# Who issues the stores, who narrows the weights, and how many staging buffers feed three chained layers on one core

## The chip, the core and the metric

The kernel runs on one core of one Trainium2 chip. The metric is the device time of one execution in microseconds. Before the change it is 679.35 us, the median of three runs (678.56 to 679.99). The core has a matrix engine (TensorE, "PE" in the profile, its weight loads "PEld"), a vector engine (VectorE, "DVE"), a scalar engine (ScalarE, "ACT"), a general engine (GpSimd, "POOL") and SyncE ("SP"), which in this kernel only issues transfers. Each engine runs its own list of instructions strictly in order and waits on semaphores for the others.

## The reference, cut to what matters

Three layers follow each other. The first is a spectral layer on x [4, 3072, 256]:

```python
X = np.fft.rfft(x, axis=1)
Yr = Xr @ w_r - Xi @ w_i + b_r
Yi = Xr @ w_i + Xi @ w_r + b_i
Yr = np.sign(Yr) * np.maximum(np.abs(Yr) - 0.01, 0.0)      # Yi the same
y = np.fft.irfft(Yr + 1j * Yi, n=3072, axis=1)
```

The second sends each of the 12,288 rows to the best of 8 experts, which keeps its first 384 rows; an expert is two matrices with a relu between (256 to 1024 to 256), and the result is scaled by the gate. Rows that no expert keeps are zero. The third layer is `h = x @ w_in; (h * sigmoid(h)) @ w_out` with 2048 hidden columns, on every row; it gives zero for a zero row. `w_in` and `w_out` arrive as 64-bit floats and are used at 32-bit precision.

## The kernel before, in words

Because the experts fill up early, the kernel transforms batch 0 and the first 1024 rows of batch 1, routes them, and takes a second, long branch only if some expert was not full. In the timed run that branch is not taken.

The order of work is this. `s1` (L347) transforms x by matmuls with a small table and stores the partial result to DRAM (`a_d`). `kphase` (L384) reloads it four frequencies at a time (`ar`), applies the second half of the transform (tile `xp`), the complex weights (`yp`), the bias and the shrinking (`y`, `cl`, on VectorE), and the first half of the inverse (`bp`), copies that out (`bo`, ScalarE) and stores it to DRAM (`b_d`). `is2` (L555) reloads it (`br`), finishes the inverse, stores the rows (`attn`), and computes the gate; `route`, `rank` and `slots` build the table of which row goes to which expert. For batch 1 only a third of that is needed (`third`), and it runs in between the first experts.

Each expert is a `first_ffn` (L960, 96 full-rate matmuls into `hp` and `y`, 8 steps) and a `second_ffn` (L997, the third layer for the expert's 384 rows, tiles `h`, `sg`, `gh`, `gl`, `o`). `experts` (L849) runs them in the order first 0, 1, 2, second 0, 1, 2, first 3, 4, second 3, 4, and so on. `gather` fetches an expert's rows (`xg`) by indirect transfers that GpSimd issues, and VectorE scales them by the gate; `turn` transposes them (`gtp`) into `xT`. `weights` (L929) brings an expert's weights in eight loads of 256 KB into staging tiles `st`.

For accuracy nearly every matmul is done as three, on a high part and a low part of each operand (`mm3`, L197). `split` (L187) makes the two parts: the high part is a rounding copy, the low part a subtraction (L191). A two-letter argument names the engines: "av" is ScalarE then VectorE, "ap" ScalarE then GpSimd. In `weights` the first matrix of an expert goes "av", the second "ap".

`narrow` (L796) turns a [128, 512] block of 64-bit floats, loaded into `nt`, into 32-bit ones in `na` with integer operations on VectorE. Its argument `bits` chooses how the sign is put back: for `w_in` ScalarE computes a sign and GpSimd multiplies by it; for `w_out` VectorE masks the sign bit (tile `nsg`) and joins it in.

The output is cleared first: `zero_out` (L203) issues one of 48 stores of 256 KB of zeros per call; finished rows are then scattered over it. `ZERO` (L40) places 16 of these calls in the second half of the spectral layer, and `experts` the others in each `second_ffn` after the first.

A scheduler with a timeline model of its own orders the instructions of each engine; `after` adds an order between two instructions without a wait. All transfers but the indirect ones are issued by SP, in one list.

Of the kernel before, what the change touches and what calls it, by code (L numbers as in the profile page):

```python
# [22 lines left out]
DFF = 2048  # L23
# [11 lines left out]
OWN = 2,  # L35
HEAD = 2
PMS = "vav"
HELD = 10
FULL = 0, 1, 3, 5, 7, 9, 11, 13, 15
ZERO = {}, {k: 2 for k in range(4, 20, 2)}, {}, {}  # L40
BIG = 65536.0
# [113 lines left out]
class Kernel:  # L155
    def __init__(self, ctx, tc, i, o):
        self.tc, self.nc, self.i, self.o = tc, tc.nc, i, o
        nc = self.nc
        cst = ctx.enter_context(tc.tile_pool(name="cst", bufs=1))
        self.dr = ctx.enter_context(tc.tile_pool(name="dr", bufs=1, space=bass.MemoryType.DRAM))  # L160
        self.ident = cst.tile([P, P], F32, name="ident")
        make_identity(nc, self.ident)
        self.table = cst.tile([P, NF, SC * E], F32, name="table")
        self.carry = cst.tile([P, E], F32, name="carry")
        nc.gpsimd.memset(self.carry, 0.0)
        nc.gpsimd.memset(self.table, 0.0)
# [7 lines left out]
        self.stored = {}  # L174

    def after(self, ins, first):
# [69 lines left out]
    def near(self):  # L246
# [4 lines left out]
        with self.stream("a", 3, "right"), self.sums("a", 2):  # L251
            self.warm()
            mix([self.s1(0, ads)], [1])
            spectra = self.kphase(0, ads, True)
            next(spectra)
            mix([self.load_tables(), spectra, self.s1(1, ads), self.ffn_in()], [8, 12, 20, 10], lead=[9, 3, 0, 0])
            with self.tc.issue_after(self.stored[1][-1]):
                self.route_consts()
            rest = self.kphase(1, ads, True)
            for _ in range(1 + HEAD):  # L260
                next(rest)
            mix([self.is2(0, (0, 1, 2), self.res)], [1])
# [122 lines left out]
    def kphase(self, b, ads, ahead=False):  # L385
# [38 lines left out]
        def shrink(k, xk, xo):  # L424
# [13 lines left out]
            v.tensor_scalar(cl, y, LAM, -LAM, ALU.min, ALU.max)  # L438
            v.tensor_tensor(cl, y, cl, ALU.subtract)
            return cl  # L440

        def back(k, bo, cl):
# [4 lines left out]
            if k % KG + 2 == KG:  # L447
                nc.sync.dma_start(out=b_d[k + 2 - KG:k + 2].rearrange("k p c -> p k c"), in_=bo)

# [5 lines left out]
        for k in range(0, NK + 6, 2):  # L455
# [6 lines left out]
            if k >= 6:  # L462
                if (k - 6) % KG == 0:
                    bo = kp.tile([P, KG, D], F32, tag="bo", name="bo")
                back(k - 6, bo, y.pop(k - 6))
            for _ in range(ZERO[b].get(k, 0)):
                self.zero_out()
            yield
# [94 lines left out]
    def is2(self, b, qbs, res):  # L563
# [17 lines left out]
        def rows(g):  # L581
# [4 lines left out]
            for z in range(0, LD, CH):  # L586
# [6 lines left out]
                nc.scalar.copy(aof[:nq, sl], pt[:nq])  # L593
            nc.sync.dma_start(out=od[:, :, g], in_=aof[:nq].rearrange("q (u c) -> q u c", c=D))
            return ao
# [199 lines left out]

    def narrow(self, src, n, bits):  # L796

# [5 lines left out]
        for sv, dv in src:  # L803
            nc.sync.dma_start(out=t[:, dv], in_=sv.bitcast(I32).rearrange("p (n z) -> p n z", z=2))
        low, high = t[:, :, 0], t[:, :, 1].bitcast(F32)
# [3 lines left out]
        nc.scalar.activation(a, high, AF.Abs, scale=UP)  # L809
        v.tensor_scalar(a, a, F_MIN, F_MAX, ALU.max, ALU.min)  # L810
        if bits:
            sg = pool.tile([P, n], I32, tag="nsg", name="nsg", bufs=1)
            v.tensor_scalar(sg, t[:, :, 1], -0x80000000, None, ALU.bitwise_and)
            v.scalar_tensor_tensor(u, u, 3, sg, ALU.logical_shift_left, ALU.bitwise_or)
            v.scalar_tensor_tensor(u, low, 29, u, ALU.logical_shift_right, ALU.bitwise_or)
        else:
            sg = pool.tile([P, n], F32, tag="nsg", name="nsg", bufs=1)
            nc.scalar.activation(sg, high, AF.Sign)
            v.tensor_scalar(u, u, 3, None, ALU.logical_shift_left)
            v.scalar_tensor_tensor(u, low, 29, u, ALU.logical_shift_right, ALU.bitwise_or)  # L820
            nc.gpsimd.tensor_tensor(a, a, sg, ALU.mult)
        return a

    def ffn_part(self, src, dst, bits):
        W = 512
        if self.i["moe2_w_in"].dtype == mybir.dt.int64:
            a = self.narrow(src, W, bits)
        else:
# [5 lines left out]
    def ffn_in(self):  # L834

        W = 512
        for q in range(8):
            h, z = q % 2, (q // 2) * W
            self.ffn_part([(self.i["moe2_w_in"][h * P:(h + 1) * P, z:z + W], slice(0, W))],
                          [self.wi[:, k, h, z:z + W] for k in range(2)], False)  # L840
            yield

    def ffn_out(self):
        for q in range(8):
            rows = [(self.i["moe2_w_out"][(2 * q + u) * P:(2 * q + u + 1) * P, :], slice(u * D, (u + 1) * D)) for u in range(2)]
            self.ffn_part(rows, [self.wo[:, k, 2 * q:2 * q + 2].rearrange("p j d -> p (j d)") for k in range(2)], True)
            yield

    def experts(self, again=False):  # L849
# [45 lines left out]
        for at, ph in enumerate(order):  # L895
# [7 lines left out]
            if ph < E:  # L903
                part = self.first_ffn(ph, xs.pop(ph), ws.pop(ph), ys)
            else:
                part = self.second_ffn(ph - E, ys.pop(ph - E))
            for _ in part:
                n += 1
                while due is not None and due <= n:
                    due = next(side, None)  # L910
                if n % 3 == 0:
                    next(fw, None)
                if ph > E and n % 2:
                    self.zero_out()
            if after < E:
                xs[after] = self.turn(xg.pop(after))

# [11 lines left out]
    def weights(self, s):  # L929
# [41 lines left out]
    def first_ffn(self, e, xT, ws, ys):  # L971
# [5 lines left out]
        for j in range(NJ + 1):  # L977
            if j < NJ:
# [6 lines left out]
                nc.scalar.activation(hh, hp, AF.Relu)  # L985
                nc.vector.scalar_tensor_tensor(hl, hp, 0.0, raw(hh), ALU.max, ALU.subtract)  # L986
                hs[j] = hh, hl
# [10 lines left out]
    def second_ffn(self, e, yT):  # L998
# [40 lines left out]
        for s_ in range(SC):  # L1039
# [56 lines left out]
```

## Time and profile before

| | |
|---|---|
| median of three runs | 679.35 us |
| profiled execution | 678.36 us, of it 676.5 us span on the engines |
| TensorE matmul | 630.6 us busy, 93% of the span, 4050 instructions |
| VectorE | 322.7 us, 48% |
| ScalarE | 316.3 us, 47% |
| GpSimd | 130.1 us, 19% |
| mean granted TensorE clock | 0.97 of full speed |
| moved by DMA | 83.1 MB, 123 GB/s over the span |

The profiled execution's own time is its span and 1.9 us around it. It lies 1.0 us under the median of the runs. TensorE is busy nearly all the time, so what counts is where it stands idle, where it runs at a lower granted clock, and what it waits for there. Matmuls overlap in the records (a new one starts before the last has drained), so the busy time of a stretch hides short pauses; the number of matmuls in it shows them. The other engines matter only where TensorE waits for them.

### The profile page before, as it was taken

Reading aid. Unit: us, or ns where it says so; the run is one execution under the profiler, and the core shown is the slowest. Engines: PE = TensorE matmul, PEld = TensorE weight load, DVE = VectorE, ACT = ScalarE, POOL = GpSimd, SP = SyncE. Lnnn points to the kernel's source line nnn. Section 1 sums busy time; section 2 is a strip of 40 time slices with the busy share of each in tenths; the row PEclk is TensorE's granted clock in tenths of the full one; section 3 lists DMA queues with packets and bytes.
Section 4 is the critical chain, followed back from the end, with each engine's and each line's share of the span. In section 5 each row is a group of like instructions: output and inputs, shape, how many; then the busy total and the mean of one; then the engine's idle time right before and its main releaser. Section 6 shows DMA issues by size and latency. Waiting matters only on the chain. (4 is left out here: it accounts for less than half of the span.)

```text
span 676.5 us, 10845 instructions
## 1 busy us (share of the span) xinstructions
PE 630.6 (93%) x4050; PEld 585.3 (87%) x4050; DVE 322.7 (48%) x637; ACT 316.3 (47%) x643; POOL 130.1 (19%) x121
## 2 busy tenths in 40 slices
PE   8699899899996989999999998999999899999993
PEld 4387789899984749899999997999999799999993
DVE  3369865675795684963222233442234442223330
ACT  4456533554233553464455444364544464544450
POOL 1036300000017531350001024220104220102001
PEclk7789999999996989999999999999999999999997
DMA  9997865786517795345000012750003320000000
GB/s 245 321 290 240 259 190 162 208 264 196 179 63 225 211 294 182 94 126 170 9 17 9 16 32 96 239 160 13 25 1 96 121 81 1 24 2 24 0 1 29
DMA packets 63542, 83.10 MB, mean 123 GB/s; under 512 B 4948, under 2 KB 53144, under 8 KB 63480
## 3 DMA queue, kind: packets, MB, share of 16 engines
q1 hardware_dynamic: 61176, 76.02, 36.7%
q0 software_dynamic: 2304, 6.29, 3.0%
q8 instruction: 34, 0.56, 0.4%
q14 instruction: 28, 0.23, 0.1%
HBM read 49.79 MB, written 32.51 MB: 122 GB/s over the span
## 5 line engine op out<-in xcount | busy, mean ns | idle before, releaser
L191 DVE TENSOR_TENSOR gl<-sg,gh 128x384 fp32r<-128x384 f32 x118 | 67.1, 572 | 163.3 <-ACT gh L183 163.1
L1019 ACT ACTIVATE sg<-h 128x384 f32<-128x384 f32 x128 | 62.5, 491 | 100.0 <-PE h L201 99.1
L200 PE MATMUL o<-wo,gl 128*128 128x256 f32 x354 | 92.7, 282 | 0.0
L201 PE MATMUL o<-wo,gh 128*128 128x256 f32 x354 | 92.4, 282 | 0.0
L199 PE MATMUL h<-yT,wi 128*128 128x384 f32 x256 | 86.1, 336 | 0.4 <-ACT yT L183 0.4
L200 PE MATMUL h<-yT,wi 128*128 128x384 f32 x256 | 86.1, 336 | 0.0
L201 PE MATMUL h<-yT,wi 128*128 128x384 f32 x256 | 85.5, 336 | 0.0
L199 PE MATMUL o<-wo,gh 128*128 128x256 f32 x354 | 73.3, 283 | 0.0
L201 PEld LDWEIGHTS o<-wo,gh 128*128 128x128 f32 x354 | 67.1, 190 | 0.0
L200 PEld LDWEIGHTS o<-wo,gl 128*128 128x128 f32 x354 | 67.0, 189 | 0.1
L183 ACT CAST gh<-sg 128x384 fp32r<-128x384 f32 x118 | 60.2, 514 | 10.5 <-PE o L201 7.4
L183 ACT CAST w<-st 128x512 fp32r<-128x512 f32 x64 | 39.2, 619 | 49.2 <-DMA st<-in_moe_w 47.0
L191 POOL TENSOR_TENSOR w<-st,w 128x512 fp32r<-128x512 f32 x32 | 42.4, 1326 | 91.0 <-ACT w L183 83.5
L199 PEld LDWEIGHTS o<-wo,gh 128*128 128x128 f32 x354 | 59.8, 188 | 0.0
L199 PE MATMUL yp<-wri,xk 128*128 128x256 f32 x188 | 55.8, 298 | 0.6 <-ACT xk L414 0.6
L200 PE MATMUL yp<-wri,xk 128*128 128x256 f32 x188 | 54.5, 290 | 2.0 <-DVE xk L415 1.5
L201 PE MATMUL yp<-wri,xk 128*128 128x256 f32 x188 | 53.2, 283 | 0.0
L986 DVE SCALAR_TENSOR_TENSOR hl<-hp,hh 128x384 fp32r<-128x384 f32 x64 | 34.6, 551 | 34.8 <-ACT hh L985 32.8
L985 ACT ACTIVATE hh<-hp 128x384 fp32r<-128x384 f32 x64 | 30.8, 489 | 41.6 <-PE y L200 18.5
L199 PEld LDWEIGHTS h<-yT,wi 128*128 128x128 f32 x256 | 48.3, 189 | 0.7 <-ACT yT L183 0.7
L199 PE MATMUL hp<-xT,w 128*128 128x384 f32 x128 | 45.6, 357 | 3.2 <-ACT xT L183 3.2
L200 PEld LDWEIGHTS h<-yT,wi 128*128 128x128 f32 x256 | 48.1, 188 | 0.0
(224 smaller groups left out, 1329.5 us busy)
## 6 DMA issues: line engine op xcount, KB each, us to landing
st<-in_moe_w SPq DMA_DIRECT2D x64, 256.0 KB, 3.0
out<-zt SPq DMA_DIRECT2D x48, 256.0 KB, 3.8
a_d<-ao SPq DMA_DIRECT2D x16, 384.0 KB, 4.0
ar<-a_d SPq DMA_DIRECT2D x12, 512.0 KB, 8.4
b_d<-bo SPq DMA_DIRECT2D x12, 512.0 KB, 3.1
br<-b_d SPq DMA_DIRECT2D x16, 384.0 KB, 4.9
xt<-in_x SPq DMA_DIRECT2D x15, 384.0 KB, 8.1
nt<-in_moe_w_in SPq DMA_DIRECT2D x8, 512.0 KB, 4.5
```

What stands on the lines that cost most here:

```text
L183: self.nc.scalar.copy(dst, src)
L191: e.tensor_tensor(dst, src, raw(hi), ALU.subtract)
L199: first = nc.tensor.matmul(out, lh, rh, start=start, stop=False)
L200: nc.tensor.matmul(out, ll, rh, start=False, stop=False)
L201: return first.ins, nc.tensor.matmul(out, lh, rl, start=False, stop=stop).ins
L985: nc.scalar.activation(hh, hp, AF.Relu)
L986: nc.vector.scalar_tensor_tensor(hl, hp, 0.0, raw(hh), ALU.max, ALU.subtract)
L1019: nc.scalar.activation(sg, hp, AF.Silu)
```

## The change

1. The stores of `b_d` and of `attn` in `is2` are issued by ScalarE in place of SP.
2. `HEAD`, two further steps of batch 1's spectra that ran ahead of `is2` for batch 0, goes.
3. No zeros are stored in the spectral layer. `experts` calls `zero_out` twice per step of `second_ffn` 0 and on every second step of the later ones.
4. `narrow` always uses the form with the sign bit on VectorE. Its loads are ordered behind the latest `ar` load, and its second operation behind the latest shrinking (`w_in`) or the latest low part of `hp` (`w_out`).
5. Four `st` buffers in place of two, and all low parts of the expert weights on VectorE.
6. `turn` of the next expert is called two steps before the end of a phase, not after it. Three `oo` buffers in place of two.

```diff
@@ near
-            for _ in range(1 + HEAD):
-                next(rest)
+            next(rest)
@@ kphase
-            v.tensor_tensor(cl, y, cl, ALU.subtract)
+            self.shrunk = v.tensor_tensor(cl, y, cl, ALU.subtract).ins
-                nc.sync.dma_start(out=b_d[k + 2 - KG:k + 2].rearrange("k p c -> p k c"), in_=bo)
+                nc.scalar.dma_start(out=b_d[k + 2 - KG:k + 2].rearrange("k p c -> p k c"), in_=bo)
-            for _ in range(ZERO[b].get(k, 0)):
-                self.zero_out()
@@ is2
-            nc.sync.dma_start(out=od[:, :, g], in_=aof[:nq].rearrange("q (u c) -> q u c", c=D))
+            nc.scalar.dma_start(out=od[:, :, g], in_=aof[:nq].rearrange("q (u c) -> q u c", c=D))
@@ narrow
-            nc.sync.dma_start(out=t[:, dv], in_=sv.bitcast(I32).rearrange("p (n z) -> p n z", z=2))
+            ins = nc.sync.dma_start(out=t[:, dv], in_=sv.bitcast(I32).rearrange("p (n z) -> p n z", z=2))
+            self.after(ins.ins, self.fetched)
-        v.tensor_scalar(a, a, F_MIN, F_MAX, ALU.max, ALU.min)
-        if bits:
+        first = v.tensor_scalar(a, a, F_MIN, F_MAX, ALU.max, ALU.min)
+        if after:
+            self.after(first.ins, after)
...
-        else:
-            sg = pool.tile([P, n], F32, tag="nsg", name="nsg", bufs=1)
-            nc.scalar.activation(sg, high, AF.Sign)
-            v.tensor_scalar(u, u, 3, None, ALU.logical_shift_left)
-            v.scalar_tensor_tensor(u, low, 29, u, ALU.logical_shift_right, ALU.bitwise_or)
-            nc.gpsimd.tensor_tensor(a, a, sg, ALU.mult)
@@ experts
-                if ph > E and n % 2:
-                    self.zero_out()
-            if after < E:
-                xs[after] = self.turn(xg.pop(after))
+                if ph >= E:
+                    for _ in range(2 if ph == E else n % 2):
+                        self.zero_out()
+                if m == last - 2 and after < E:
+                    xs[after] = self.turn(xg.pop(after))
@@ weights
-                st = self.mq.tile([P, 2, D], F32, tag="st", name="st", bufs=2)
+                st = self.mq.tile([P, 2, D], F32, tag="st", name="st", bufs=4)
-                self.split("ap" if m else "av", w[:, 0], w[:, 1], st)
+                self.split("av", w[:, 0], w[:, 1], st)
@@ second_ffn
-            oo = self.mc.tile([P, D], F32, tag="oo", name="oo", bufs=2)
+            oo = self.mc.tile([P, D], F32, tag="oo", name="oo", bufs=3)
```

Three places show how the lists of instructions move. The first is VectorE's list where the spectra of batch 1 end and the first expert begins: `dsts` is the last table of `slots`, `xg` are gathered rows being scaled, `w_...` low parts of expert weights, `xT` the low part of the first transposed rows. Before:

```order
L758 CAST dsts<-slbs 128x9
L436 TENSOR_TENSOR y<-yp,bias 128x512
L438 TENSOR_SCALAR cl<-y 128x512
L439 TENSOR_TENSOR cl<-y,cl 128x512
L191 TENSOR_TENSOR w_2190<-st,w_2190 128x512
L959 TENSOR_SCALAR xg<-xg,gws 128x256 x3
L191 TENSOR_TENSOR xT<-gtp,xT 128x384 x2
```

Now, from the third low part after `dsts` (the first two are those of `w_2166` and `w_2171`):

```order
L190 TENSOR_TENSOR w_2176<-st,w_2176 128x512
L952 TENSOR_SCALAR xg<-xg,gws 128x256
L434 TENSOR_TENSOR y<-yp,bias 128x512
L190 TENSOR_TENSOR w_2181<-st,w_2181 128x512
L952 TENSOR_SCALAR xg<-xg,gws 128x256
L436 TENSOR_SCALAR cl<-y 128x512
L952 TENSOR_SCALAR xg<-xg,gws 128x256
L190 TENSOR_TENSOR w_2186<-st,w_2186 128x512
L437 TENSOR_TENSOR cl<-y,cl 128x512
L190 TENSOR_TENSOR w_2191<-st,w_2191 128x512
L952 TENSOR_SCALAR xg<-xg,gws 128x256
L190 TENSOR_TENSOR xT<-gtp,xT 128x384
```

One low part of weights stood ahead of the first `xT`, now six do, and the last shrinking has moved in between them.

The second is SP's list of transfers. Before, a piece among the loads of the first experts, where zeros stand between weight loads and row stores:

```order
L538 DMA attn_69<-ao_2429 32x512 x4
L943 ISA
L943 DMA st<-in_moe_w 128x2x256
L208 DMA out<-zt 256x1x256 x5
L943 ISA
```

Now, after the first weight load of expert 3 (`flagi` is the flag that decides the second branch, `nt` the last blocks of `w_out`):

```order
L936 DMA st<-in_moe_w 128x2x256
L1056 TENSOR_LOAD flagi
L1056 ISA x2
L800 DMA nt<-in_moe_w_out 128x512 x2
L207 DMA out<-zt 256x1x256 x45
L936 ISA
L936 DMA st<-in_moe_w 128x2x256
```

The zeros have left the loads of the first three experts; 45 of the 48 stand in one row ahead of seven loads of expert 3.

The third is VectorE's list in the spectra of batch 0 (numbers kept; `xk`, `y` and `cl` belong to the spectra, `na`, `nt` and `nsg` to the narrowing of `w_in`). Before:

```order
L413 TENSOR_TENSOR xk_473<-xp_474,xk_473 128x4x128
L810 TENSOR_SCALAR na_713<-na_713 128x512
L415 TENSOR_TENSOR xk_473<-xk_473,xp_474 128x4x64
L436 TENSOR_TENSOR y_508<-yp_483,bias_264 128x512
L819 TENSOR_SCALAR na_713<-na_713 128x512
L438 TENSOR_SCALAR cl_510<-y_508 128x512
L820 SCALAR_TENSOR_TENSOR na_713<-nt_711,na_713 128x512
L439 TENSOR_TENSOR cl_510<-y_508,cl_510 128x512
```

Now:

```order
L434 TENSOR_TENSOR y_505<-yp_480,bias_264 128x512
L436 TENSOR_SCALAR cl_507<-y_505 128x512
L811 TENSOR_SCALAR nsg_464<-nt_459 128x512
L437 TENSOR_TENSOR cl_507<-y_505,cl_507 128x512
L184 COPY ao1_520<-ps1_522 96x512
L807 TENSOR_SCALAR na_461<-na_461 128x512
L812 SCALAR_TENSOR_TENSOR na_461<-na_461,nsg_464 128x512
L411 TENSOR_TENSOR xk_538<-xp_539,xk_538 128x4x128
```

The narrowing is spread over more steps of the spectra, and each block now has an operation (`nsg`) that reads a freshly loaded `nt` between two operations of the spectra.

## Rows read from the trace of the kernel before

**Rows 1.** Windows: stretch in us, then length, busy time (instructions) by engine, clock, DMA.

```profile
0.00:44.00 44.00, 33.18 (x109) 20.46 (x110) 18.96 (x34) 22.41 (x43) 7.75 (x19) 0.77 0.96 286
44.00:100.00 56.00, 53.41 (x347) 44.33 (x346) 44.73 (x74) 28.51 (x53) 17.28 (x12) 1.00 0.75 236
192.00:220.00 28.00, 20.47 (x112) 17.49 (x111) 19.12 (x44) 10.47 (x25) 15.14 (x13) 0.82 0.53 155
236.00:258.00 22.00, 18.88 (x78) 13.28 (x78) 15.74 (x25) 10.25 (x20) 8.66 (x7) 0.84 0.98 301
212.00:310.00 98.00, 92.94 (x481) 80.89 (x481) 66.12 (x142) 49.25 (x98) 40.21 (x32) 0.93 0.63 188
310.00:400.00 90.00, 90.00 (x642) 90.00 (x641) 24.46 (x44) 43.93 (x92) 7.21 (x7) 1.00 0.08 26
```

**Rows 2.** TensorE's waits, whole run: total us, times, longest us.

```profile
PE y L199 <- ACT hh L985: 4.0, 3, 1.5
...
PE hp L199 <- ACT xT L183: 3.2, 3, 1.4
PE xp L401 <- DMA ar<-a_d: 2.6, 1, 2.6
```

**Rows 3.** Windows in the later first_ffn phases, same columns.

```profile
404.00:408.00 4.00, 4.00 (x25) 4.00 (x24) 2.44 (x5) 1.26 (x3) 0.91 (x1) 1.00 0.29 98
412.00:428.00 16.00, 12.10 (x66) 10.66 (x66) 7.07 (x13) 7.05 (x15) 7.83 (x7) 1.00 0.36 111
524.00:536.00 12.00, 9.12 (x50) 8.13 (x49) 5.33 (x10) 5.72 (x13) 2.57 (x2) 1.00 0.44 131
```

**Rows 4.** ScalarE's timeline, 419 to 421 us: start, length, what, idle before.

```profile
419.52 0.62 ACT L183 CAST w<-st 128x512 fp32r<-128x512 f32 x1 [2.83 <-DMA st<-in_moe_w]
420.05 0.47 ACT L183 CAST xT<-gtp 128x384 fp32r<-128x384 f32 x1
```

**Rows 5.** Tile st: min/median/max ns, first and last start; landing in us.

```profile
L191 DVE TENSOR_TENSOR w<-st,w x32: 674/692/1172, 205.1 to 617.3; 128x512 fp32r<-128x512 f32 x32
L191 POOL TENSOR_TENSOR w<-st,w x32: 1263/1292/1817, 209.9 to 622.1; 128x512 fp32r<-128x512 f32 x32
...
DMA to landing us min/median/max: 2.6/3.0/6.0
```

**Rows 6.** SP's timeline of transfers: start, length, what.

```profile
25.83 0.99 SPq L804 DMA_DIRECT2D nt<-in_moe_w_in  x2
27.75 1.39 SPq L395 DMA_DIRECT2D ar<-a_d  x2
...
68.22 0.38 SPq L448 DMA_DIRECT2D b_d<-bo  x1
...
201.79 4.59 SPq L943 DMA_DIRECT2D st<-in_moe_w  x3
```

**Rows 7.** Tile nsg: min/median/max ns of two narrowing operations on VectorE.

```profile
L813 DVE TENSOR_SCALAR nsg<-nt x8: 414/426/1457, 73.2 to 249.0; 128x512 int32<-128x512 int32 x8
L814 DVE SCALAR_TENSOR_TENSOR na<-na,nsg x8: 676/689/694, 73.7 to 249.8; 128x512 int32<-128x512 int32 x8
```

**Rows 8.** SP's own waits, whole run.

```profile
SPq L448 <- ACT bo L183: 38.2, 10, 8.8
```

**Rows 9.** VectorE's timeline, 208.5 to 210 us.

```profile
208.66 0.35 DVE L959 TENSOR_SCALAR xg<-xg,gws 128x256 f32<-128x256 f32 x1 [2.25 <-DMA xg<-attn,srcs]
209.55 1.79 DVE L959 TENSOR_SCALAR xg<-xg,gws 128x256 f32<-128x256 f32 x1 [0.53 <-DMA xg<-attn,srcs]
```

**Rows 10.** GpSimd's timeline from 209.9 us.

```profile
209.90 1.28 POOL L191 TENSOR_TENSOR w<-st,w 128x512 fp32r<-128x512 f32 x1
```

**Rows 11.** SP's timeline, two runs of zero stores.

```profile
253.27 3.45 SPq L208 DMA_DIRECT2D out<-zt  x5
...
305.72 7.09 SPq L208 DMA_DIRECT2D out<-zt  x9
```

**Rows 12.** VectorE's waits, whole run.

```profile
DVE nsg L813 <- DMA nt<-in_moe_w_out: 7.5, 3, 3.6
```

More of the change, by code (lines that the diff above doesn't have):

```diff
@@ L35 @@
 OWN = 2,
-HEAD = 2
 PMS = "vav"
@@ L39 @@
 FULL = 0, 1, 3, 5, 7, 9, 11, 13, 15
-ZERO = {}, {k: 2 for k in range(4, 20, 2)}, {}, {}
 BIG = 65536.0
@@ L174, in __init__ @@
         self.stored = {}
+        self.again, self.evicted = False, None
     def after(self, ins, first):
@@ L794, in wide, with narrow @@
         self.wi = mw.tile([P, 2, 2, DFF], FR, name="wi")
-    def narrow(self, src, n, bits):
+    def narrow(self, src, n, after):
         nc, pool = self.nc, self.mn
@@ L809, in narrow, with ffn_part @@
         nc.scalar.activation(a, high, AF.Abs, scale=UP)
-        v.tensor_scalar(a, a, F_MIN, F_MAX, ALU.max, ALU.min)
-        if bits:
-            sg = pool.tile([P, n], I32, tag="nsg", name="nsg", bufs=1)
-            v.tensor_scalar(sg, t[:, :, 1], -0x80000000, None, ALU.bitwise_and)
-            v.scalar_tensor_tensor(u, u, 3, sg, ALU.logical_shift_left, ALU.bitwise_or)
-            v.scalar_tensor_tensor(u, low, 29, u, ALU.logical_shift_right, ALU.bitwise_or)
-        else:
-            sg = pool.tile([P, n], F32, tag="nsg", name="nsg", bufs=1)
-            nc.scalar.activation(sg, high, AF.Sign)
-            v.tensor_scalar(u, u, 3, None, ALU.logical_shift_left)
-            v.scalar_tensor_tensor(u, low, 29, u, ALU.logical_shift_right, ALU.bitwise_or)
-            nc.gpsimd.tensor_tensor(a, a, sg, ALU.mult)
+        first = v.tensor_scalar(a, a, F_MIN, F_MAX, ALU.max, ALU.min)
+        if after:
+            self.after(first.ins, after)
+        sg = pool.tile([P, n], I32, tag="nsg", name="nsg", bufs=1)
+        v.tensor_scalar(sg, t[:, :, 1], -0x80000000, None, ALU.bitwise_and)
+        v.scalar_tensor_tensor(u, u, 3, sg, ALU.logical_shift_left, ALU.bitwise_or)
+        v.scalar_tensor_tensor(u, low, 29, u, ALU.logical_shift_right, ALU.bitwise_or)
         return a
-    def ffn_part(self, src, dst, bits):
+    def ffn_part(self, src, dst, after):
         W = 512
         if self.i["moe2_w_in"].dtype == mybir.dt.int64:
-            a = self.narrow(src, W, bits)
+            a = self.narrow(src, W, after)
         else:
@@ L839, in ffn_in @@
             self.ffn_part([(self.i["moe2_w_in"][h * P:(h + 1) * P, z:z + W], slice(0, W))],
-                          [self.wi[:, k, h, z:z + W] for k in range(2)], False)
+                          [self.wi[:, k, h, z:z + W] for k in range(2)], None if self.again else self.shrunk)
             yield
@@ L845, in ffn_out @@
             rows = [(self.i["moe2_w_out"][(2 * q + u) * P:(2 * q + u + 1) * P, :], slice(u * D, (u + 1) * D)) for u in range(2)]
-            self.ffn_part(rows, [self.wo[:, k, 2 * q:2 * q + 2].rearrange("p j d -> p (j d)") for k in range(2)], True)
+            self.ffn_part(rows, [self.wo[:, k, 2 * q:2 * q + 2].rearrange("p j d -> p (j d)") for k in range(2)], self.evicted)
             yield
@@ L903, in experts @@
             if ph < E:
-                part = self.first_ffn(ph, xs.pop(ph), ws.pop(ph), ys)
+                part, last = self.first_ffn(ph, xs.pop(ph), ws.pop(ph), ys), F // P
             else:
-                part = self.second_ffn(ph - E, ys.pop(ph - E))
-            for _ in part:
+                part, last = self.second_ffn(ph - E, ys.pop(ph - E)), DFF // P + 1
+            for m, _ in enumerate(part):
                 n += 1
@@ L985, in first_ffn @@
                 nc.scalar.activation(hh, hp, AF.Relu)
-                nc.vector.scalar_tensor_tensor(hl, hp, 0.0, raw(hh), ALU.max, ALU.subtract)
+                self.evicted = nc.vector.scalar_tensor_tensor(hl, hp, 0.0, raw(hh), ALU.max, ALU.subtract).ins
                 hs[j] = hh, hl
```

## The prediction

> **What bounds the kernel now.** I read the windows by stage first [rows 1]. From 310 to 400 us TensorE is busy for the whole stretch at full clock; no change can win anything there. It loses time in four places, and there is nothing else to win: the start (0 to 44, 33.2 us busy, granted clock 0.77), the first gather (192 to 220, 20.5 of 28, clock 0.82), a hole at 236 to 258 (18.9 of 22, clock 0.84, DMA busy 98%), and the two later `first_ffn` phases [rows 3]. In the stretches at 0.77 to 0.84 part of the time was spent at the lower of the two levels (1.2 GHz, not 2.4). Idle time and the lower level stand in the same windows, so an idle microsecond there may be paid twice, once as idle and again as slow matmuls.
>
> The second view is TensorE's list of waits [rows 2]: it stands for `hh` (4.0 us in 3), `xT` (3.2 in 3) and once 2.6 us for `ar`. The first two have ScalarE as releaser, so I looked at what ScalarE did before: a weight cast that had waited 2.83 us for the DMA of its `st` tile, with the `xT` cast queued behind it [rows 4]. The engine is not slow; it is held in order behind a late load.
>
> The third is SP's list [rows 6, 8, 11]: two `nt` loads go ahead of the first `ar`, three `st` issues take 4.59 us where zeros share the queues, and SP stands 38.2 us in ten waits for `bo`.
>
> **The change, part by part.** The sum is made against the profiled execution, 678.4 us (span 676.5 and 1.9 around it); the median is 1.0 higher, and I add that at the end.
>
> *Staging buffers and low parts (later phases).* A `st` buffer is held for the landing (3.0 us), ScalarE's cast (0.62) and the low part. For the second matrix the low part is GpSimd's, 1.29 us [rows 4, 5]: 4.9 us, and with two buffers one load per 2.46 us. Eight loads feed 96 matmuls, which at full pace (25 in 4 us) last 15.4 us, so one load is wanted every 1.9 us. The loads are the limit, and the holes are where they should be: 412 to 428 has 66 matmuls where 100 would fit, 524 to 536 has 50 of 75 [rows 3]. That is 34 and 25 missing at 0.16 us, 9.4 us in all; the idle time alone is 3.9 and 2.9, 6.8 us. After the change a buffer is held 3.0 + 0.62 + 0.69 = 4.3 us, and with four of them a load can come every 1.08 us, well under 1.9. What is late next is nothing on this path: VectorE is 44% busy in these windows (7.07 of 16), and four more low parts per expert add 2.8 us. I take 8 us of the 9.4 (a few matmuls at the edges are missing only by the count), range 5 to 9.4. The earlier `turn` and the third `oo` buffer act on the same holes and are counted here.
>
> *236 to 258, and the phases around it.* The nine zero stores (2.4 MB) issued by SP while DMA is busy 98% [rows 1, 11] go. Reachable are the idle 3.1 us and, at most, (1 - 0.84) x 22 = 3.5 us of clock: 6.6. Against it, VectorE gets here 12 low parts that were GpSimd's (12 x 0.69 = 8.3 us) and four more `w_out` blocks, each five operations between 0.43 and 0.69 us [rows 7], 2.2 us at least, so 9 us: 66 us busy of 98 becomes 83, 85%. An engine in order at 85% is late now and then: each low part of `hp` or `xT` that comes 0.7 us late behind a narrowing costs TensorE that, and seven such come to 5 us. I take a gain of 2, nearer to the middle, range -5 to +6.6.
>
> *Start, 0 to 44.* Loads of `w_in` now stand behind the latest `ar` load, so the two `nt` ahead of it (1 MB) [rows 6] go. At the 286 GB/s of this stretch [rows 1] 1 MB is 3.7 us; the wait for `ar` that it can shorten is 2.6 us [rows 2], and behind it (1 - 0.77) x 44 = 10 us went to the slow clock, most of it in the unavoidable first loads. I take 3, range 0 to 5.
>
> *44 to 100.* TensorE idles 2.6 us here [rows 1]. VectorE loses four `w_out` blocks (9 us) and gains the sign-bit form for `w_in`. Two of that form's operations are in rows 7, 1.1 us together; the shift and the join of the old form stay, so about one operation per block more, 0.43 to 0.69. The stores on ScalarE free SP of its 38.2 us of waiting [rows 8], during which the `ar` and `br` loads behind a store could not be issued. ScalarE pays the issue: 0.38 us a store where SP does it [rows 6], up to 0.7 by the `ar` and `st` loads there. Three stores of `b_d` stand in this stretch and 12 in the run, with 8 of `attn`: 1 to 2 us here, at most 14 in the run, on an engine that is 51% busy (28.5 of 56), hidden beside TensorE's 53 us of matmuls, and on the path if the copy behind a store is the one TensorE waits for. I take a gain of 1, range -3 to +2.6.
>
> What the row shows here is head-of-line waiting, 38.2 us on SP, up to 8.8 at a time [rows 8]. The Trainium skill (DMA: Bandwidth & Descriptors, "Issuing engines are not separate DMA queues") says that starting transfers from several engines saves only the sequencer's time for starting them, usually small beside the transfer. By that rule this term is 0 and the sum 1 us less. The rule does not count a wait ahead of the issue, and that is what the row has; which is right, the waits for `ar` and `br` after the change would show.
>
> *First gather, 192 to 220.* Idle 7.5 us and (1 - 0.82) x 28 = 5 us of clock [rows 1], the largest hole. It is made by the chain routing table, row gather, scaling, transposing, and the change doesn't touch its length except at two points. The scaling of one `xg` took 1.79 us in place of 0.35 while GpSimd did a low part beside it [rows 9, 10]; without GpSimd's work that is 1.4 us won. Against it, six low parts (6 x 0.69 = 4.1 us) stand on VectorE ahead of the first `xT` where one stood, and the fifth and sixth need a second turn of the buffers: from 201.8 (the first of the issues in rows 6), two turns of 4.3 us end at 210.4, and the last scaling before was done at 211.3 (209.55 + 1.79 [rows 9]). So they just fit, and if the loads land late (6.0 at worst, [rows 5]) `xT` is late by up to 4. I take 0.5, range -4 to +4. Two steps of batch 1's spectra that ran ahead of `is2` are no longer there (`HEAD`); they are moved, not removed, and are matmuls either way.
>
> *Zeros.* 45 stores stand on SP in one row ahead of seven loads of expert 3. At 7.09 us for 9 [rows 11] their issue lasts 35 us. DMA is busy 8% from 310 to 400 [rows 1], and those weights are wanted from about 400. Issued from about 310 they are through by 345, and the transfers (45 x 0.26 MB at 301 GB/s, 39 us) by 350: no cost. If SP got to them only after 355, the loads behind would come after 394 and each further microsecond would be one on TensorE.
>
> The sum: 8 + 2 + 3 + 1 + 0.5 = 14.5 us. 678.4 - 14.5 = 663.9, and with the 1.0 to the median 664.9 us.
>
> **The rivals.** *Only the weights.* The two later phases win 8, and the early terms come to nothing, since one hole there is filled by another: the start is bound by loads, the gather by its chain, and VectorE takes back what the DMA gives. 679.35 - 8 = 671.4. For it: the weights are the one term in which cause, period and hole agree; against it: the wait for `ar` has a plain cause in SP's order.
>
> *The early holes close and the clock stays up.* If the start, the hole at 236 and 44 to 100 all reach their upper bounds' better half, the clock does not fall either: 9 + 5 + 4 + 2 + 2.4 = 22.4, 657. All upper bounds together are 9.4 + 6.6 + 5 + 2.6 + 4 = 27.6, 651.8. For it: idle time and slow clock stand together in all three windows; against it: VectorE at 85% in the middle one.
>
> *VectorE held by fresh loads (slower).* The sign-bit operation `nsg` reads a freshly loaded `nt`, and now stands in order between operations of the spectra in all 16 blocks. Where it waited before it was 2.5 us each (7.5 in 3 [rows 12]). Sixteen such waits hold VectorE 40 us, and behind it stand `y`, `cl` and the low part of `xk`, for which TensorE waits. The kernel is slower than before from the point where over 14.5 + 1.4 = 15.9 us of these, 1.0 us per block, reach TensorE; if half of them do, 20 us, it is 664.9 + 20 = 684.9. Against it: most of the loads before had landed when the operation came (3 waits), and the order of the loads behind `ar` moves them away from the busiest moment, but later as well.
>
> **How the numbers follow.** The forecast 0.52; only the weights 0.24; the early holes 0.16; VectorE held 0.08, of which 0.06 is slower and 0.02 ends within the bound. What can be told from no change is 0.2%, 1.4 us. So faster 0.92, same 0.02, slower 0.06. The range that holds 8 in 10: its low end is the third case, 657, and 1 below it; its high end is the second, 671.4, with 3.6 for the low bounds of the early terms (the -4 of the gather). 656 to 675.
>
> **What would show it.** Weights: 100 matmuls in 16 us in the later `first_ffn` phases, and no wait for `hh` or `xT` behind ScalarE. Start: no 2.6 us wait for `ar`, and `nt` behind it on SP. Middle: DMA under 0.9 where it was 0.98, clock over 0.9, and VectorE near 85%; waits of TensorE for VectorE's low parts there would show my -5. Gather: all `xg` scalings at 0.35, and the first `xT` behind six low parts at no later time than before. Zeros: one row of 45 on SP, ended before 355. I am wrong if `nsg` shows waits in the spectra that TensorE's waits for `xk` or `y` repeat, or if ScalarE's issues of stores stand ahead of copies for which TensorE waits.

## The result and the profile after

The changed kernel takes 660.82 us (median of 4, 660.42 to 663.07), the kernel before 678.95 in the same comparison. The ratio is 0.974 with a 95% interval of 0.971 to 0.977. The forecast was 664.9 in a range of 656 to 675: 14.5 us of gain forecast, 17.6 us found between the two profiled spans (676.5 and 658.9).

The page of the changed kernel, in the 40 slices (here 16.5 us each): TensorE, its granted clock, DMA.

```profile
PE   7689999999985999899999999999999999999993
...
PEclk7799999999987999999999999999999999999998
DMA  8997935983127874799500014400004300000000
```

Two holes are left, the start and the first gather (slices 12 and 13). The windows that answer to [rows 1] and [rows 3] (length, then PE, PEld, DVE, ACT, POOL, granted clock, DMA share, GB/s):

```profile
0.00:44.00 44.00, 32.92 (x133) 20.49 (x134) 15.74 (x28) 19.82 (x38) 2.54 (x15) 0.84 0.94 275
44.00:100.00 56.00, 55.83 (x373) 47.34 (x372) 48.35 (x88) 26.53 (x52) 10.91 (x8) 1.00 0.72 229
192.00:220.00 28.00, 20.96 (x99) 17.73 (x98) 18.54 (x52) 9.39 (x18) 10.82 (x10) 0.82 0.68 206
236.00:258.00 22.00, 22.00 (x123) 19.04 (x122) 16.34 (x34) 10.55 (x21) 2.56 (x2) 1.00 0.55 167
212.00:310.00 98.00, 95.00 (x540) 84.20 (x539) 66.48 (x154) 47.75 (x96) 17.63 (x15) 1.00 0.77 245
404.00:420.00 16.00, 15.59 (x90) 15.03 (x89) 10.10 (x21) 8.62 (x18) 3.06 (x3) 1.00 0.48 139
```

From 44 to 100 no hole is left, at 236 to 258 TensorE is busy throughout at full clock, and a later phase has 90 matmuls in 16 us. TensorE's list of waits over the whole run, as in [rows 2], now begins with other names:

```profile
PE c3t L308 <- DMA c<-in_tab: 5.8, 3, 4.1
PE gtp L960 <- issue: 5.5, 2, 4.6
PE y L200 <- DVE hl L979: 2.9, 4, 1.1
...
PE xp L399 <- DMA ar<-a_d: 0.3, 1, 0.3
```

The waits for `hh` and `xT` behind a cast are nearly gone, that for `ar` too; that for `hl` on VectorE now leads them. The 4.6 us of `gtp` under "issue" are the first gather: the first transpose starts at 203.13 us, just behind the first scaled rows (203.07).

Fixed windows compare different work once the two kernels have drifted apart. So I also took, from TensorE's timeline, the start of the first matmul of five pieces and subtracted: *until hp*: from the start to the first `hp`; *middle*: from there to the first `h`; *next*: the three `second_ffn`, to the `hp` of expert 3; *later 1* and *later 2*: `first_ffn` 3, 4 and 5, 6, each up to the next `h`. The stretches between and behind these last two are the same in all kernels to 0.1 us, up to the last matmul. In us; the medians are those of each kernel's own comparison, in which the kernel before stood at 677.6 to 679.6:

| kernel | median | until hp | middle | next | later 1 | later 2 |
|---|---|---|---|---|---|---|
| before | 678.95 | 212.4 | 81.8 | 105.8 | 37.0 | 36.0 |
| changed | 660.82 | 206.2 | 77.5 | 105.7 | 33.8 | 33.1 |
| b_w: before, four buffers, low parts on VectorE | 664.28 | 212.9 | 76.0 | 105.1 | 32.5 | 31.9 |
| b_av2: before, low parts on VectorE | 672.35 | 213.8 | 78.9 | 107.8 | 35.7 | 34.1 |
| u_st2ap: changed, two buffers, GpSimd's low parts | 678.37 | 206.9 | 87.4 | 105.3 | 37.8 | 34.9 |
| u_av2: changed, two buffers | 661.05 | 203.5 | 76.8 | 106.0 | 33.9 | 33.3 |
| u_ap4: changed, GpSimd's low parts | 666.04 | 206.1 | 78.5 | 108.4 | 34.8 | 33.0 |
| u_turn: changed, late turn, two `oo` | 661.32 | 205.0 | 78.3 | 106.0 | 32.6 | 31.9 |
| u_zero: changed, zeros as before | 670.01 | 213.9 | 81.0 | 105.1 | 34.3 | 33.0 |
| u_sp: changed, stores on SP | 662.09 | 208.4 | 76.6 | 104.4 | 33.7 | 33.1 |
| u_narrow: changed, `narrow` as before | 677.93 | 212.4 | 82.9 | 110.2 | 33.8 | 33.0 |
| n_form: changed, old sign form for `w_in` | 667.67 | 214.0 | 77.5 | 105.1 | 33.6 | 33.0 |
| best1: changed, late turn, two buffers | 669.56 | 206.7 | 83.1 | 106.0 | 34.3 | 35.7 |
| best2: as best1, with `HEAD` | 669.62 | 205.3 | 80.8 | 106.7 | 34.2 | 33.0 |

The changed kernel gained 6.2 us until the first `hp`, 4.2 in the middle, 3.2 and 3.0 in the later phases, and 0.9 behind the last matmul. In the first column kernels with the same early code (changed, u_ap4, u_av2, u_turn, u_st2ap, best1) lie between 203.5 and 206.9: one profile of an early piece is good to some 3 us. In the two last columns kernels with the same weights and `turn` (changed, u_sp, u_narrow, n_form) agree to 0.2 us, but where holes are left they need not (best1 and best2: 35.7 and 33.0). Each row has one profiled execution beside the median of several: for b_av2, u_zero and best1 it was the slowest (676.23, 671.77 and 671.33 us), for u_turn, u_sp and best2 the fastest (658.11, 660.88 and 664.35).

### The profile page after: what moved, and what is told of

The parts are those of the page before. It is cut to its first block, busy times and chain, and to the rows that moved or that the text cites. A ratio compares the mean times of both kernels' runs of the same rounds, so it can differ in the third digit from the quotient of the medians.

```text
span 658.9 us, 10803 instructions
## 1 busy us (share of the span) xinstructions
PE 623.1 (95%) x4050; PEld 581.2 (88%) x4050; DVE 330.5 (50%) x677; ACT 312.0 (47%) x635; POOL 76.0 (12%) x81
## 5 line engine op out<-in xcount | busy, mean ns | idle before, releaser
L190 DVE TENSOR_TENSOR gl<-sg,gh 128x384 fp32r<-128x384 f32 x118 | 65.5, 558 | 165.8 <-ACT gh L182 165.2
L200 PE MATMUL o<-wo,gh 128*128 128x256 f32 x354 | 93.1, 282 | 0.0
L198 PE MATMUL o<-wo,gh 128*128 128x256 f32 x354 | 75.1, 283 | 0.0
L190 DVE TENSOR_TENSOR w<-st,w 128x512 fp32r<-128x512 f32 x64 | 44.3, 696 | 23.5 <-ACT w L182 19.3
L198 PEld LDWEIGHTS h<-yT,wi 128*128 128x128 f32 x256 | 48.3, 189 | 0.7 <-ACT yT L182 0.7
L199 PEld LDWEIGHTS h<-yT,wi 128*128 128x128 f32 x256 | 48.1, 188 | 0.3 <-issue 0.3
L200 PEld LDWEIGHTS h<-yT,wi 128*128 128x128 f32 x256 | 48.1, 188 | 0.0
```

The lines of the kernel that those rows point to most:

```text
L190: e.tensor_tensor(dst, src, raw(hi), ALU.subtract)
L198: first = nc.tensor.matmul(out, lh, rh, start=start, stop=False)
L199: nc.tensor.matmul(out, ll, rh, start=False, stop=False)
L200: return first.ins, nc.tensor.matmul(out, lh, rl, start=False, stop=stop).ins
```

## The experiments

### The weights: buffers, engines, or both

u_st2ap undoes the whole weight edit in the changed kernel, u_ap4 and u_av2 a half of it each; b_w does it alone in the kernel before.

```diff
-                st = self.mq.tile([P, 2, D], F32, tag="st", name="st", bufs=4)
+                st = self.mq.tile([P, 2, D], F32, tag="st", name="st", bufs=2)     # u_st2ap, u_av2
-                self.split("av", w[:, 0], w[:, 1], st)
+                self.split("ap" if m else "av", w[:, 0], w[:, 1], st)              # u_st2ap, u_ap4
```

> The changed kernel with two st buffers and GpSimd's low parts for the second matrix, as before. If the period of the buffers made the holes (4.9 us over 2 buffers, 2.46 us a load, against 1.9 to 2.1 us wanted), the holes of the later first_ffn phases are back, about 3 us each, and with the relief that VectorE gets in the middle phases the time is 666 to 669 us. If the earlier turn and the third oo buffer closed them, or the moved zeros did, the time stays within 2 us of the changed kernel's 660.8.

> The changed kernel with four st buffers, but the second matrix's low parts on GpSimd. By the period (4.9 us over 4 buffers, 1.2 us a load) the later phases have no holes: 660 to 662 us, and as VectorE has 8.3 us less in the middle phases it may be up to 2 us faster than the changed kernel. If GpSimd itself was the limit (1.29 us a part, in order behind its indirect transfers), part of the holes comes back: 663 to 667 us.

> The changed kernel with two st buffers, but all low parts on VectorE. By the period (4.3 us over 2 buffers, 2.15 us a load, just above the 1.9 to 2.1 us wanted) small holes stay: 662 to 666 us, most of the 6 us of the later phases still there. If the engine alone mattered, 661 us; if the number of buffers alone did, 667 us, as with GpSimd.

> The kernel before with four st buffers and all low parts on VectorE, and nothing else of the change. The theory: the two later phases gain 6 to 8 us and the rest stays: 671 to 673 us. The rival is that the parts need each other (without the early turn xT still comes late, and the low parts that VectorE takes cost in the middle phases): 674 to 678 us.

u_st2ap took 678.37 us (ratio to before 1.000, 0.997 to 1.004): with this one edit undone, all the others together are worth nothing. In the table the 5.5 us until the first `hp` stay, and the middle, 5.7 us longer than before, gives them back. I expected 666 to 669. b_w took 664.28 us (0.978, 0.970 to 0.986), 14.2 us faster than before, where I expected 671 to 673. u_ap4 took 666.04 (0.981, 0.972 to 0.989), u_av2 661.05 (0.975, 0.965 to 0.984).

u_av2 took what I had named for the case that the engine alone matters: in the changed kernel two buffers in place of four cost nothing that can be measured. u_ap4 fell into the range for GpSimd as the limit, but its interval overlaps that of u_av2, and of the 4.5 us between its span and the changed kernel's 2.7 lie in *next*, 1.0 in the middle and 0.9 in the later phases. So GpSimd as the limit of the later phases is not shown, nor what makes *next* longer.

The later phases behave as the period said: 37.0 and 36.0 us in the kernel before, 32.5 and 31.9 in b_w, 8.6 us in the two. The middle gains 5.7 us more in b_w, and there I had looked at the wrong thing. b_w still stores its zeros where the kernel before does, nine in this window in both. Its window at 236 to 258:

```profile
236.00:258.00 22.00, 19.72 (x97) 14.77 (x97) 16.08 (x30) 9.80 (x20) 3.84 (x3) 1.00 0.95 298
```

DMA is nearly as full as before (0.95 and 298 GB/s, against 0.98 and 301 in [rows 1]), yet the clock is 1.00 in place of 0.84 and 97 matmuls stand where 78 did (123 in the changed kernel). So zeros beside a full DMA were not enough to make this hole. ScalarE's waits in the middle (first `hp` to first `h`) show that weights were short there; before, the first row, in b_w no wait of this kind is among the longest:

```profile
ACT w L183 <- DMA st<-in_moe_w: 12.5, 10, 2.4
```

```profile
ACT na L809 <- DMA nt<-in_moe_w_out: 7.0, 3, 3.7
ACT hh L985 <- PE y L200: 5.4, 6, 1.1
ACT wo L183 <- DVE na L815: 5.3, 4, 2.6
```

It is the shortage of the later phases once more, but the way from it to TensorE is not the same. From 236 to 260 us in the kernel before, no wait of TensorE is behind a weight cast:

```profile
PE ps L533 <- DMA br<-b_d: 1.2, 1, 1.2
PE lg L551 <- DVE aT L547: 0.9, 1, 0.9
PE y L201 <- DVE hl L986: 0.7, 1, 0.7
```

The granted clock is 1.00 from 244 to 248 us, 0.58 from 248 to 252, after these waits, and 0.56 from 252 to 256; in b_w TensorE waits 2.1 us for `br` in the same stretch, in pieces of at most 0.9, and the clock stays at 1.00. So the weight edit takes most of this hole away in the kernel before; by which wait is not shown, and u_narrow and u_zero (below) have the same weight edit and middles of 82.9 and 81.0 us. In u_st2ap the shortage shows on SP. TensorE's waits and SP's in its middle (205 to 300 us):

```profile
PE ps L529 <- DMA br<-b_d: 5.4, 3, 2.6
```

```profile
SPq L534 <- ACT ao L532: 10.8, 4, 3.3
SPq L936 <- POOL w L190: 9.0, 7, 2.2
```

SP stands for `ao`, the rows that are to be stored, and for GpSimd's low part until an `st` buffer is free, and the reload `br` of batch 1's last spectra is issued behind both. That the reload's wait and SP's belong together is read from the order of the list; no run takes the one away alone.

### One word, and two buffers without the early turn

```diff
-                self.split("ap" if m else "av", w[:, 0], w[:, 1], st)
+                self.split("av", w[:, 0], w[:, 1], st)                  # b_av2, on the kernel before
```

> The kernel before with one word changed: all low parts of the expert weights on VectorE, the two st buffers kept. With four buffers as well it gained 14 us. If the period is what counts (4.3 us over 2 buffers, 2.15 us a load, against 2.46 with GpSimd), most of it is here too: 664 to 667 us, the later phases 32.5 to 34 us each. If GpSimd's low parts and the number of buffers each had a share, 669 to 673 us.

b_av2 took 672.35 us (0.990, 0.985 to 0.994): half of b_w's gain, as expected where both edits have a share. The two-buffer period of 2.15 us a load (4.3 over 2) is still too long: the later phases last 35.7 and 34.1 us, and the wait of [rows 4] is shorter but there. TensorE's waits from 380 to 560 us, and ScalarE's timeline:

```profile
PE hp L199 <- ACT xT L183: 2.9, 2, 1.5
```

```profile
416.77 0.62 ACT L183 CAST w<-st 128x512 fp32r<-128x512 f32 x1 [1.33 <-DMA st<-in_moe_w]
418.41 0.62 ACT L183 CAST w<-st 128x512 fp32r<-128x512 f32 x1 [1.02 <-DMA st<-in_moe_w]
418.93 0.85 ACT L183 CAST xT<-gtp 128x384 fp32r<-128x384 f32 x2
```

So with `turn` late, the sum of the two later phases is 73.0 us at a period of 2.46 us, 69.8 at 2.15, and 64.5 at 1.08 (b_w): the time follows the period. u_av2 had 67.2 with two buffers; its `turn` is early, and TensorE no longer waits for an `xT` behind those casts. At a period of 2.46 us the early `turn` does not help: u_st2ap has 72.7. Nor does `xT` always fall behind a late cast at 2.15: best2, below, has a late `turn`, two buffers and 67.2, with 0.4 us of waits for `xT`, where best1, which differs from it by `HEAD` alone, has 70.0 and 2.7 us. What decides it is not shown.

### The early turn

```diff
-                if m == last - 2 and after < E:
-                    xs[after] = self.turn(xg.pop(after))
+            if after < E:
+                xs[after] = self.turn(xg.pop(after))          # u_turn; oo again with bufs=2
```

> The changed kernel with turn of the next expert after the end of a phase and two oo buffers, as before. In the profile of the kernel before with the weight edit alone, the two stretches from the first hp of a later phase to its second_ffn last 32.5 and 32.0 us; in the changed kernel 33.8 and 33.1, with two waits for hl of 0.9 us behind xg scalings that wait for their gather. If the early turn causes that, this kernel is 1.5 to 2.5 us faster than the changed one, 658 to 659.5 us. If the early turn was needed for xT (1.5 us waits before), it is 1 to 3 us slower, 662 to 664 us.

The later phases last 32.6 and 31.9 us, as in b_w, against 33.8 and 33.1: with four buffers the early `turn` (or the third `oo` buffer, undone with it) costs 1.2 us twice. VectorE in the changed kernel, where expert 3 begins (start, length, what, idle before):

```profile
391.89 0.35 DVE L952 TENSOR_SCALAR xg<-xg,gwt 128x256 f32<-128x256 f32 x1 [0.98 <-DMA xg<-attn,srct]
393.25 0.35 DVE L952 TENSOR_SCALAR xg<-xg,gwt 128x256 f32<-128x256 f32 x1 [1.00 <-DMA xg<-attn,srct]
393.51 0.55 DVE L979 SCALAR_TENSOR_TENSOR hl<-hp,hh 128x384 fp32r<-128x384 f32 x1
```

and in u_turn:

```profile
392.00 0.35 DVE L952 TENSOR_SCALAR xg<-xg,gwt 128x256 f32<-128x256 f32 x1 [0.99 <-DMA xg<-attn,srct]
392.27 0.55 DVE L979 SCALAR_TENSOR_TENSOR hl<-hp,hh 128x384 fp32r<-128x384 f32 x1
393.36 0.35 DVE L952 TENSOR_SCALAR xg<-xg,gwt 128x256 f32<-128x256 f32 x1 [0.54 <-DMA xg<-attn,srct]
```

In the first, `hl` stands behind a third scaling that waits for its gather; in the second it goes ahead of it, and TensorE's waits for `hl` from 380 to 560 us fall from 1.8 us to 0.4. This points at the `turn`. Yet the median, 661.32 us (0.978, 0.972 to 0.984), doesn't show the 2.4 us: the runs spread over more than that (658.1 to 667.6). The phases show a gain, the whole does not.

### Zeros, stores, narrowing

> The changed kernel with the zeros stored where they were: 16 in batch 1's spectra, the others in the second_ffn phases after the first. With the weight edit alone the middle stretch (first hp to first h) already fell from 81.8 to 76.1 us, zeros in place, against 77.5 in the changed kernel. So the theory that the low parts made that hole expects no loss here: 659.5 to 662 us. The prediction's step, that the zeros beside loads at 98% DMA made it, expects 2 to 4 us more: 663 to 665 us.

> The changed kernel with the stores of b_d and attn issued by SP again. If SP's standing for bo (38.2 us in ten waits before) delayed the ar and br loads behind it, the 3 us that the changed kernel gained between 44 and 100 us go, in part or all: 662 to 664 us. By the rule that another issuing engine saves only the issue, nothing changes: 660 to 661.5 us.

> The changed kernel with narrow as before: sign by ScalarE and GpSimd for w_in, no order of its loads behind ar, none of its second operation. If the order of the loads gave the gain at the start (the first xp came 2.2 us and the first yp 3.3 us earlier), that is lost, and part of the 3 us of 44 to 100 if the form and its order behind the shrinking matter there: 663 to 667 us. If the gain of the start was only a drift, 660 to 662 us.

> The changed kernel with the old sign form for w_in (ScalarE's sign, GpSimd's product), but the new order of loads and second operations kept. With all of narrow undone the first hp came at 212.4 us in place of 206.2, and the end 16 us later. If the order made these gains, this is 660 to 662.5 us with the first hp at 205 to 207.5; if the form did (VectorE held beside GpSimd's products, ScalarE's extra operation), 665 to 678 us with the first hp at 210 or later.

u_zero puts the `ZERO` table and the old rule in `experts` back. It took 670.01 us (0.987, 0.982 to 0.991), 9 us more than the changed kernel and outside both ranges: the first `hp` comes 7.7 us later and the middle is 3.5 us longer. The largest single wait is at the first gather, TensorE's list from 180 to 300 us:

```profile
PE gtp L962 <- DVE xg L954: 8.3, 3, 8.0
```

No zeros were issued near it (16 up to 149 us, the next nine from 281 on). Of the 7.7 us, 4.7 are there by the last `xp` and 3.0 come in the gather, where the first rows are scaled 6.9 us after their issue, with four weight loads issued within 2 us of it. How much of this the zeros themselves cost, and how much the scheduler's other list, stays open.

u_sp (`nc.scalar` back to `nc.sync` in both stores) took 662.09 us (0.979, 0.974 to 0.984), not told apart from the changed kernel. SP again stands for `bo`, and longer than in [rows 8]:

```profile
SPq L446 <- ACT bo L182: 56.1, 11, 10.0
```

56 us of SP's standing cost here at most the 2.2 us by which the first `hp` is later, less than such a piece scatters. The Trainium skill (DMA: Bandwidth & Descriptors, "Issuing engines are not separate DMA queues") says that another issuing engine saves only the time of the issue, usually small beside the transfer. This run agrees, though the waits that the rule leaves out are there; no run has the stores on ScalarE in the kernel before.

u_narrow (the old `narrow`, without the new orders) took 677.93 us (1.001, 0.998 to 1.003): this edit undone also loses everything. The first `hp` is at 212.4, as before the change, the middle takes 82.9 us and *next* 110.2, 5.4 and 4.5 us more than in the changed kernel. DMA is 87 to 100% busy from 240 to 300 us:

```profile
240.00:260.00 20.00, 16.85 (x70) 12.25 (x69) 12.39 (x22) 8.16 (x17) 4.27 (x3) 0.85 0.87 270
260.00:280.00 20.00, 20.00 (x119) 18.90 (x119) 13.03 (x43) 8.49 (x19) 0.00 (x0) 0.98 0.96 309
280.00:300.00 20.00, 20.00 (x119) 19.79 (x119) 11.68 (x33) 6.18 (x13) 6.54 (x7) 1.00 1.00 325
```

But TensorE loses nothing where DMA is fullest: from 260 to 300 us it does 238 matmuls, the changed kernel 233. It loses from 240 to 260, with 70 in place of 117 and the clock at 0.85, and what it waits for there is `br` (4.5 us in three from 236 to 260). So four buffers and VectorE's low parts do not by themselves keep the middle short. The scheduler had drawn the zeros among the weight loads, from 242 us on in pieces of 1 to 15, where the changed kernel issues 45 in one row and then the loads:

```profile
271.56 37.20 SPq L207 DMA_DIRECT2D out<-zt  x45
309.01 7.33 SPq L936 DMA_DIRECT2D st<-in_moe_w  x7
```

n_form keeps the new orders and gives `w_in` the old form:

```diff
+            sg = pool.tile([P, n], F32, tag="nsg", name="nsg", bufs=1)
+            nc.scalar.activation(sg, high, AF.Sign)
+            v.tensor_scalar(u, u, 3, None, ALU.logical_shift_left)
+            v.scalar_tensor_tensor(u, low, 29, u, ALU.logical_shift_right, ALU.bitwise_or)
+            nc.gpsimd.tensor_tensor(a, a, sg, ALU.mult)
```

It took 667.67 us (0.983, 0.978 to 0.988), in the range that I had set for the form. The first `xp` comes at 33.1 us, as in the changed kernel (32.8; before 35.0): that gain is the order of the loads. The first `hp` comes at 214.0, so the rest of the early gain is gone. From the first `yp` to the middle of the spectra (the 76th matmul `xp`) n_form takes 42.0 us, the changed kernel 40.5, the one before 43.5 and u_narrow 43.7: in these profiles order and form have about half of that gain each. The other kernels with the new form and order take 40.1 to 41.4, so the share of the form is hardly more than the scatter. More is lost around 103 us, where TensorE waits 3.7 us for the reload of batch 1. SP issues it 5.4 us later than in the changed kernel, behind the last stores of `a_d` (n_form, then changed):

```profile
88.30 10.35 SPq L380 DMA_DIRECT2D a_d<-ao  x2
...
101.63 1.43 SPq L393 DMA_DIRECT2D ar<-a_d  x2
```

```profile
81.45 11.90 SPq L380 DMA_DIRECT2D a_d<-ao  x2
...
96.22 1.49 SPq L393 DMA_DIRECT2D ar<-a_d  x2
```

u_narrow has the old form too, and not this wait; so it is no property of the form, but of the lists that the scheduler made with it. What in them makes `a_d` late stays open.

### Two tries for a faster kernel

best1 is the changed kernel with `turn` late and two `st` buffers, best2 the same with the two steps of `HEAD` back.

> The changed kernel with turn late as before and two st buffers in place of four (three oo buffers kept). The later phases should last 32 to 33 us each, as with turn late alone, and the start and the spectra be as in the changed kernel: 656 to 659.5 us. If two buffers need the early turn, the later phases last 34 us or more and the time is 661 to 664 us.

> As the last one, and with the two further steps of batch 1's spectra ahead of is2 again. If their removal is what the first gather lost in the changed kernel (0.9 us more from the last xp to the first hp), this is 1 to 2 us faster than the last one; if it is no more than a shift of matmuls, the same within 1 us; if it holds up the routing of batch 0, 2 to 4 us slower by the first hp.

best1 misses both of its ranges: 669.56 us (0.984, 0.979 to 0.988). Its later phases have the holes of b_av2 again (34.3 and 35.7 us), and the middle is 83.1. The case for it was that u_av2 and u_turn each stayed at 661 us; together they take away both the early `turn` and the two further buffers. best2 took 669.62 (0.984, 0.979 to 0.990), the same within 1 us, as expected of a mere shift of matmuls: with `HEAD` the first `hp` is 1.4 us earlier, within the scatter, and the median does not move. No kernel run here is shown to beat the changed one.

## Why the prediction was right, and which steps were not

*Weights in the later phases (8 us).* The mechanism held. The edit alone gains 8.6 us there, by b_w. The changed kernel gets 6.2, since the early `turn`, which I had counted as help, takes 2.4 back; it has 90 and 93 matmuls in 16 us (404 to 420 and 510 to 526), not 100. All 64 low parts are on VectorE at the duration used ([rows 5] has 692 ns):

```profile
L190 DVE TENSOR_TENSOR w<-st,w x64: 675/688/1132, 198.6 to 604.6; 128x512 fp32r<-128x512 f32 x64
```

*236 to 258 and the phases around it (2 us, -5 to +6.6).* The middle gained 4.2, inside the range, but the step that put the hole down to zeros beside a full DMA failed: in b_w the DMA is nearly as full, with the same nine zeros, and most of the hole closes. The weight edit, which I had counted in the later phases alone, takes 5.7 us out of the middle there. It is not the only condition, since u_narrow and u_zero have it too, and long middles; through which wait it acts stays open. My counterweight, VectorE at 85% and late, did not come: from 212 to 310 us it is busy 66.5 us, not 83, and TensorE's waits for `hl` in the middle are 1.9 us. In this stretch VectorE has 19 low parts where it had 14, not 12 more, since five more are done before it and the loads of expert 3 stand behind the zeros; it has two `w_out` blocks more, not four (only two lay before 212 us, and a block is four operations, not five); and beside less work of GpSimd (17.6 us in place of 40.2) single operations are shorter: the six scalings of `xg` by `gwt` took 0.74 us on average, now 0.35. The zeros are not free for all that; put back into the changed kernel, they cost 9 us with the lists that go with them.

*Start (3 us).* Right: the first `xp` is 2.2 us and the first `yp` 3.3 us earlier, the wait for `ar` falls from 2.6 to 0.3, and n_form, with the order alone, keeps it. Not all waits there fell: those for the tables (`c3t`) are 5.8 us, 4.0 before.

*44 to 100 (1 us, -3 to +2.6).* The gain by then is 3 us beyond the start, past my upper end. By u_narrow all of it is the narrowing; by n_form at least about half is the order, and the sign form, which I had booked as a cost, costs nothing. Nor had VectorE four `w_out` blocks to lose here: two lay in this stretch. SP's freedom from `bo`, which I had booked as the gain, gives next to nothing in the changed kernel (u_sp takes 40.8 us for the piece that takes the changed kernel 40.5).

*First gather (0.5 us, -4 to +4).* From the last `xp` to the first `hp` it takes 30.7 us, 29.8 before: 0.9 lost, but kernels with the same early code take 29.4 to 31.2, so neither gain nor loss is shown. The first scaling came late, for a reason that I had only half. GpSimd's first gather and VectorE's first scaling in the changed kernel:

```profile
196.55 1.21 POOL L948 DMA_INDIRECT xg<-attn,srcs  x1 [8.06 <-DVE dsts L754]
```

```profile
202.10 0.69 DVE L190 TENSOR_TENSOR w<-st,w 128x512 fp32r<-128x512 f32 x1 [0.64 <-ACT w L182]
202.71 0.36 DVE L952 TENSOR_SCALAR xg<-xg,gws 128x256 f32<-128x256 f32 x1
```

That is 6.2 us from issue to scaling, and the scaling starts without a wait for its rows: it stands in VectorE's list behind a third low part, which waits for ScalarE's cast. In the kernel before it was 4.0 us, and there the rows came last:

```profile
202.08 1.20 POOL L955 DMA_INDIRECT xg<-attn,srcs  x1 [8.06 <-DVE dsts L758]
```

```profile
206.06 0.35 DVE L959 TENSOR_SCALAR xg<-xg,gws 128x256 f32<-128x256 f32 x1 [0.27 <-DMA xg<-attn,srcs]
```

With two buffers, in u_av2, it is 3.3 (194.73 to 198.06). With four buffers four weight loads are issued around the first gather in place of two, and three low parts stand before the scaling, one before the change and two in u_av2. The scaling itself takes 0.34 to 0.36 us each time, as forecast.

*Rivals.* Only the weights: b_w shows that this alone is 14.2 us, not 8. The early holes close: until the first `h` the kernel gained 10.4 us, midway between the 6.5 of the forecast and the 13.4 of this rival; 44 to 100 and the hole at 236 did close and the clock there is 1.00, but at the gather it is 0.82 as before. VectorE held by fresh loads: `nsg` did wait, 5.2 us in 4 and 4.6 in 1 where I had priced 40, and until 180 us TensorE waited 0.2 us in all for `xk`, and not for `cl`.

*Zeros on SP.* The 45 are issued by 308.8, far from 355, and *next* takes 105.7 us, 105.8 before: no cost, as forecast.

The total was 3 us short: the step that failed gave the middle to the zeros and set VectorE's load against it, while the weights alone had 5.7 us there. That it was no further off is in part luck: the weights (-1.8) and the gather (-1.4) fell short, the middle (+2.2) and 44 to 100 (+2.0) came out above. Nor do the parts add up as the sum supposed: the weights undone, or the narrowing undone, each loses all, and the weights alone give 14 of 18.

## What to carry to other kernels

Where one engine casts from staging buffers in order, work out the period of a buffer (landing, cast, low part) over their number and compare it with the rate at which loads are wanted in every phase that uses them, not in the one with the plainest hole: a full DMA beside a hole need not be its cause. Undoing one part of a change tells what it is worth in that company only; try it alone as well before adding such numbers up. Once a lookahead (here the further buffers) has cured a wait, ask whether a second cure for the same wait still earns its place, as the early `turn` did not.

## What was not expected of the hardware

DMA at 95% and 298 GB/s stood beside TensorE at full clock (b_w, 236 to 258 us). The first indirect gather of 128 rows came 3.3 us (u_st2ap), 4.0 (before) and 6.9 us (u_zero) after its issue, read where the scaling waits for it; two, two and four loads of 256 KB were issued within 2 us of it. The number of loads alone does not set this: u_turn has four as well, and the median of its first gathers is 4.2 us to landing, in u_zero 6.5.
